# Pooled attention into a GELU MLP: value products in concurrent tiles of the PE array, and loads, pooling and DMA transposes at other places

## The chip, the cores and the metric

The kernel runs on one core of a Trainium2 chip. A core has five engines that each work through their own instruction stream in order and meet at semaphores: TensorE (PE, matrix products; its weight loads are shown apart as PEld), VectorE (DVE), ScalarE (ACT), GpSimd (POOL) and SyncE (SP, which here only starts transfers). Transfers run on 16 DMA engines. The metric is device time in microseconds (us), the median of several runs; lower is better.

## The reference

Two stages follow each other. Attention has 8 batches, 8 heads, 576 positions and 64 dimensions per head; keys and values are first averaged over blocks of 8 positions, so each head has only 72 pooled keys:

```python
k_p = k.reshape(B, H, Sp, pool, D).mean(axis=3)
v_p = v.reshape(B, H, Sp, pool, D).mean(axis=3)
scores = scale * np.matmul(q, k_p.transpose(0, 1, 3, 2))
scores = scores - np.max(scores, axis=-1, keepdims=True)
attn = np.exp(scores)
attn = attn / (np.sum(attn, axis=-1, keepdims=True) + 1e-09)
return np.matmul(attn, v_p).astype(np.float32)
```

Its output, with the heads side by side, is a matrix of 4608 rows and 512 columns, which goes through an MLP with a hidden width of 2048:

```python
h = x @ w_in
g = 0.5 * h * (1.0 + np.tanh(c * (h + 0.044715 * h * h * h)))
return (g @ w_out).astype(np.float32)
```

Inputs and output are float32. The kernel multiplies in bf16 and accumulates in float32.

## The kernel before

**Groups.** The 4608 rows are cut into nine groups of 512. Groups 0 to 7 are the first 512 positions of each batch; group R (number 8) collects the last 64 positions of all eight batches. They run in the order 0 to 6, R, 7 (`seq`). A group's MLP has a first product (16 blocks `fo` of the hidden width, each 4 matmuls over `ko`, then GELU on ACT into `gT`: `hidden`, L296 and L298) and a second product (4 row blocks `r` of 16 matmuls: `output`, L301; a copy `osb` on DVE and a store: `finish`).

**Steps and hooks.** The order of work is written out by hand. In `mlp` every matmul of a group has a step number: 0 to 63 are the first product, 64 to 127 the second. The attention of the next group is hung at step numbers with `at(hooks, step, function, ...)`, and each engine and queue gets its instructions in that order. A step only fixes the order within an engine's stream: an engine whose operands are ready runs ahead of PE, and one that waits holds up what stands behind it in its own stream. `mlp_first` does the same for group 0 with a longer numbering.

**K and V.** A tile `kv` (three buffers, shared with the staging of the weights) holds 9 chunks of 128 pooled positions by 8 by 64, in float32. The 576 = 8 x 72 pooled rows of K fill chunks 0 to 3 and the lower half of chunk 4; those of V the upper half of chunk 4 and chunks 5 to 8. `pool` adds the 8 neighbours in three halvings on DVE (L128, L129, L130) into `kvb`, in bf16. K is doubled (`dup_k`), transposed (on PE for groups 0 and 1, by a DMA transpose from SP later, L178) into `kT`, and `k_spread` copies it into `kbd`, in which each pair of heads is block-diagonal. V goes through `spread_v` on POOL (five multiplications by a mask of zeros and 0.125, L148) into `vbd`: 128-row blocks in which the columns of both heads of a pair are masked by row.

**q, scores, softmax.** q is loaded (L110), cast to `q_b` on POOL (L80) and transposed by a DMA transpose from SP (L199) into `qT`. `scores` has four matmuls per block of 128 rows, one for each pair of heads, of 144 columns (L208); for R it uses two 64-column tiles for each (L213). `exps` is one exponential on ACT (L221). `norm` sums (L228), takes the reciprocal (L230) and multiplies into `eb` (L231), on DVE for blocks 0, 2 and 3 and on POOL for block 1. Each block of `eb` is transposed into `eT` by a DMA transpose from SP (L244).

**Value products.** `values` multiplies `eT` with `vbd`. Since 72 rows per head do not fit blocks of 128, each pair of heads touches two blocks (`PARTS`): 8 full-array matmuls of 512 columns for a group (L266), 64 of 64 columns for R (L272), 16 of 256 for group 0 (L255). ACT copies the result into `xT` (L78) at step 121; seven matmuls of the second product remain behind it before the next group's first product reads `xT`.

**Where the preparation stands.** For the group stage `n_`, with next group `n` and the one after it `n2`: K and V of `n` are pooled and K is transposed in the first product (L178), scores and softmax are in the second, q of `n2` is loaded at step 57 (L570), and at step 91 q of `n2` is cast and transposed and K and V of `n2` are loaded.

**Queues.** All transfers but one go out from SP, in order: loads (L91, L93, L98, L110, L114), transposes and stores (L280, L284).

The softmax here doesn't subtract the row's maximum and nothing guards it: scores larger than these inputs give would overflow.

## Time and profile before

The median of three runs is 301.29 us (301.25 to 301.42). The execution that was profiled took 301.36 us; its span, from the first to the last instruction, is 299.3 us.

| Row of the profile | Engine | Busy us | Mean ns of one |
|---|---|---|---|
| second product L301, x560 | PE | 128.6 | 379 |
| first product L296, x640 | PE | 127.6 | 358 |
| value products L266, x56 | PE | 13.2 | 379 |
| scores L208, x128 | PE | 13.2 | 226 |
| GELU L298, x160 | ACT | 88.4 | 555 |
| spread of V L148, x40 | POOL | 21.2 | 553 |
| sums of the softmax L228, x36 | DVE | 26.5 | 736 |

The page gives busy time and idle time by groups of equal instructions. A matmul's 379 ns is its own latency; they overlap, and one of 512 columns starts 0.216 us after the other. The chain of waits is followed back from the last instruction to what released each step, and is the view for what sets the time. The timeline lists instructions by start, with their durations and, in brackets, the idle time of the engine before them and what ended it; PEq and SPq are the sequencers that issue. Transfers are listed with their time from issue to landing. Two waits of POOL and SP that the change touches stand in the list of waits: POOL's `vbd` on DVE's `kvb` 113.4 us, SP's `eT` transposes on DVE's `eb` 74.1 us. Idle time of an engine that is not on the chain costs nothing by itself.

### The profile page before, as it was taken

The page shows a single profiled execution, that of the slowest core. Times are in us where ns is not written, and L with a number is a line of the kernel's source. Part 1 is how long each engine was busy: PE and PEld are TensorE (multiplying, and loading weights), DVE is VectorE, ACT ScalarE, POOL GpSimd, SP SyncE. Part 2 cuts the span into 40 slices and gives each one's busy share as a digit, 9 for nine tenths or more (in the row PEclk, how much of TensorE's full clock was granted, in tenths as well). Part 3 has the DMA queues.
Part 4 walks back from the last instruction along what each step waited for, and adds up shares of the span by engine and source line. Part 5 has one row for each costly group of instructions (what it writes and reads, how often), then busy time and mean ns, then how long its engine had stood idle before and what let it go on. Part 6 is the DMA issues. An engine that isn't in the chain of part 4 may idle for free.

```text
span 299.3 us, 4581 instructions
## 1 busy us (share of the span) xinstructions
PE 290.7 (97%) x1734; PEld 151.6 (51%) x1734; DVE 146.7 (49%) x241; ACT 158.2 (53%) x242; POOL 55.5 (19%) x71
## 2 busy tenths in 40 slices
PE   7869999999999999999999999999999999999996
PEld 7748844445444544454445444544444544444444
DVE  6895769164706570648073807381639100920012
ACT  1477783667157715672477246724773267426500
POOL 3252033230400240024012400240024000100000
PEclk9999999999999999999999999999999999999999
DMA  7999997995699459947993599049944800351012
GB/s 235 357 387 338 384 350 132 343 279 158 135 279 250 145 127 271 269 146 126 261 297 134 119 249 301 4 107 249 276 147 101 164 36 2 79 114 37 0 70 70
DMA packets 73221, 56.32 MB, mean 188 GB/s; under 512 B 45808, under 2 KB 55408, under 8 KB 73200
## 3 DMA queue, kind: packets, MB, share of 16 engines
q1 hardware_dynamic: 73056, 55.98, 68.2%
q8 instruction: 13, 0.21, 0.3%
q10 hardware_dynamic: 144, 0.07, 0.1%
q14 instruction: 8, 0.07, 0.1%
HBM read 36.70 MB, written 9.44 MB: 154 GB/s over the span
## 4 chain that ended last, share of the span: by engine, by line
PE 91%; DMA 3%; DVE 2%; SPq 1%; POOL 1%; issue 0%; POOLq 0%
PE mm L296 41%; PE mm L301 41%; PE xo L266 4%; DMA q_sb<-in_q_dram 3%; PE sc L208 2%; PE mm L329 1%; POOL eb L231 1%; SPq L98 1%; PE xo L272 1%; PE tp L193 1%; PE sc L213 0%; DVE w_in_b L80 0%; PE tp L240 0%; DVE w_out_b L80 0%; POOL q_b L80 0%; PE xo L255 0%
## 5 line engine op out<-in xcount | busy, mean ns | idle before, releaser
L301 PE MATMUL mm<-w_out_b,gT 128*128 128x512 bf16 x560 | 128.6, 379 | 0.5 <-DVE w_out_b L80 0.5
L296 PE MATMUL mm<-xT,w_in_b 128*128 128x512 bf16 (+1 forms) x640 | 127.6, 358 | 0.5 <-DVE xT L80 0.5
L298 ACT ACTIVATE gT<-mm 128x512 bf16<-128x512 f32 (+1 forms) x160 | 88.4, 555 | 47.0 <-PE mm L296 45.9
L296 PEld LDWEIGHTS <-w_in_b 128*128 128x128 bf16 x640 | 62.2, 98 | 62.6 <-issue 0.5
L301 PEld LDWEIGHTS <-gT 128*128 128x128 bf16 x560 | 53.4, 98 | 59.7 <-DVE w_out_b L80 0.7
L80 DVE COPY osb<-mm 128x512 f32<-128x512 f32 (+2 forms) x37 | 24.3, 658 | 62.9 <-PE mm L301 60.8
L78 ACT CAST xT<-xo 128x1024 bf16<-128x1024 f32 (+1 forms) x18 | 16.6, 966 | 56.8 <-PE xo L266 49.1
L228 DVE TENSOR_REDUCE den<-e 128x8 f32<-128x576 f32 x36 | 26.5, 736 | 38.0 <-ACT e L221 37.9
L148 POOL TENSOR_TENSOR vbd<-kvb,vmask 128x256 bf16<-128x256 bf16 (+2 forms) x40 | 21.2, 553 | 113.5 <-DVE kvb L130 113.4
L128 DVE TENSOR_TENSOR kv<-kv 128x1024 f32<-128x1024 f32 (+3 forms) x20 | 22.4, 1118 | 29.7 <-DMA kv<-in_v_dram 27.7
L231 DVE TENSOR_TENSOR eb<-e,r 128x576 bf16<-128x576 f32 x28 | 27.2, 970 | 1.0
L221 ACT ACTIVATE e<-sc 128x576 f32<-128x576 f32 x36 | 22.5, 650 | 9.6 <-ACT e L221 4.0
L231 POOL TENSOR_TENSOR eb<-e,r 128x576 bf16<-128x576 f32 x8 | 10.1, 1266 | 71.5 <-ACT e L221 41.1
L80 POOL CAST q_b<-q_sb 128x2048 bf16<-128x2048 f32 (+1 forms) x7 | 15.0, 2147 | 4.1 <-DMA q_sb<-in_q_dram 4.1
L208 PEld LDWEIGHTS <-qT 128*128 128x128 bf16 x128 | 10.1, 98 | 7.0 <-ACT qT L78 0.6
L208 PE MATMUL sc<-kbd,qT 128*128 128x144 bf16 x128 | 13.2, 226 | 0.2 <-ACT qT L78 0.2
L266 PE MATMUL xo<-eT,vbd 128*128 128x512 bf16 x56 | 13.2, 379 | 0.0
L129 DVE TENSOR_TENSOR kv<-kv 128x512 f32<-128x512 f32 (+3 forms) x20 | 12.8, 640 | 0.7
L410 PE MATMUL warm<-identb 128*128 128x128 bf16 x112 | 9.1, 249 | 1.4 <-POOL vmask L398 1.4
L494 ACT ACT_TABLE_LOAD x8 | 10.3, 1283 | 0.1
L80 DVE COPY kbd<-kTd 64x288 bf16<-64x288 bf16 x12 | 5.6, 467 | 8.3 <-DMA kTd<-kvb 8.2
L314 ACT ACT_TABLE_LOAD x7 | 9.0, 1283 | 0.1
(55 smaller groups left out, 99.5 us busy)
## 6 DMA issues: line engine op xcount, KB each, us to landing
out_dram<-osb SPq DMA_DIRECT2D x31, 256.0 KB, 6.7
kv<-in_k_dram SPq DMA_DIRECT2D x7, 1024.0 KB, 6.5
q_sb<-in_q_dram SPq DMA_DIRECT2D x7, 1024.0 KB, 5.9
kv<-in_v_dram SPq DMA_DIRECT2D x7, 1024.0 KB, 9.9
w_in_s<-in_moe_w_in_dram SPq DMA_DIRECT2D x4, 1024.0 KB, 13.0
w_out_s<-in_moe_w_out_dram SPq DMA_DIRECT2D x4, 1024.0 KB, 13.8
out_dram<-osb SPq DMA_DIRECT2D x9, 128.0 KB, 2.3
kv<-in_k_dram SPq DMA_DIRECT2D x2, 512.0 KB, 3.9
```

The costliest lines, as they stand in the source:

```text
L78: eng.copy(out=out, in_=in_)
L80: eng.tensor_copy(out=out, in_=in_)
L128: add(out=t[:, :, 0:4, :], in0=t[:, :, 0:4, :], in1=t[:, :, 4:8, :], op=ALU.add)
L148: eng.tensor_tensor(out=vbd[p0:128, b, n0:n1, :].rearrange("p (c r) (hh d) -> p c (r hh) d", c=max(m, 1), d=D), in0=kvb[p0:128, 4 + c0:4 + ...
L208: nc.tensor.matmul(out=o, lhsT=qT[:, j, pr, :], rhs=kbd[:, g, pr].rearrange("d hh s -> d (hh s)"), start=True, stop=True)
L221: nc.scalar.activation(out=e.rearrange("p (x h) s -> p x (h s)", x=2), in_=sc[:, :, 0:4 * Sp], func=ACT.Exp, scale=1.0 / 64.0)
L228: nc.vector.reduce_sum(out=den, in_=e, axis=AX.X)
L231: eng.tensor_tensor(out=eb[:, j, 128 * 5 - W:].rearrange("p (h s) -> p h s", s=Sp), in0=e, in1=r.unsqueeze(2).to_broadcast([128, H, Sp]), ...
L266: nc.tensor.matmul(out=xo[:, i, :], lhsT=vbd[:, g, n, :], rhs=eT[:, :, c, :], start=(x == 0), stop=(x == 1))
L296: nc.tensor.matmul(out=hp[:, 0:c1 - c0], lhsT=w_in_b[:, ko, fo * 128:(fo + 1) * 128], rhs=st[g]["xT"][:, ko, c0:c1], start=(ko == 0), stop ...
L298: nc.scalar.activation(out=gT[:, fo, c0:c1], in_=hp[:, 0:c1 - c0], func=ACT.Gelu_apprx_tanh)
L301: nc.tensor.matmul(out=o, lhsT=gT[:, fo, r * 128:(r + 1) * 128], rhs=w_out_b[:, fo, :], start=(fo == 0), stop=(fo == FO - 1))
```

## The change

**Value products.** V is laid out by head: `vb` holds for each of 4 chunks the first 64 pooled rows of two heads, one in partitions 0 to 63, one in 64 to 127. The last 8 pooled rows of every head go to every second partition of chunk 4, mixed with the last 64 rows of K in the others. A group's product is then four matmuls on 32 rows of the array (`values_rem`), which start the sum, and eight on 64 x 64 tiles (`values_main`), four of which lie on different quarters of the array. `spread_v` is one multiplication on POOL, into `vrem`. The factor 0.125, which was in the mask, moves into the eviction (`evict`), half of which is on ACT and half on DVE. R's product does the same for each batch, in columns of 64. `eb` has another order, which takes a second, small multiplication in `norm`; `scores` writes its heads in two runs of 72 for each; the first product takes `ko` in the order 0, 2, 1, 3.

**Loads and pooling.** From group 3 on, K and V are loaded and pooled in the stage before the last one, two groups ahead: loaded at step 3 and pooled at 34 and 54 (in stage 1: 24, 92 and 107). q is loaded at 30 (57 in stage 1) and cast at 68 instead of 91. K's DMA transpose moves to step 92 (107 in stage 1), `k_spread` to step 10 of the stage after (56 for group 2, which keeps its loads and its K transpose where they were). V is now loaded in two transfers, one for each half of the partitions. R's q moves from step 92 to 110.

**The start.** The two halves of chunk 4 are loaded from ACT's queue, and the second half of V too, behind a small DVE memset that follows the first pooling.

```diff
     def load_half(b, which, eng):
+        dst = st[b]["kv"][:, 4].rearrange("(m i) pl d -> i m (pl d)", i=2)
         if which == "v":
-            eng.dma_start(out=st[b]["kv"][64:128, 4], in_=rows(v, b)[0:64])
-        else:
-            eng.dma_start(out=st[b]["kv"][0:64, 4], in_=rows(k, b)[512:576])
-    def load_main(b, which, c0, c1, eng):
-        t, w0, b0 = (k, 0, 0) if which == "k" else (v, 64, 5)
-        src = rows(t, b)[w0 + 128 * c0:w0 + 128 * c1].rearrange("(c p) pl d -> p c pl d", p=128)
-        eng.dma_start(out=st[b]["kv"][:, b0 + c0:b0 + c1], in_=src)
+            src = v[b].rearrange("h (sp pl) d -> h sp (pl d)", pl=8)[:, 64:72]
+            eng.dma_start(out=dst[0], in_=src)
+        else:
+            eng.dma_start(out=dst[1], in_=rows(k, b)[512:576].rearrange("m pl d -> m (pl d)"))
+    def load_main(b, which, c0, c1, eng, halves=(0, 1)):
+        if which == "k":
+            src = rows(k, b)[128 * c0:128 * c1].rearrange("(c p) pl d -> p c pl d", p=128)
+            eng.dma_start(out=st[b]["kv"][:, c0:c1], in_=src)
+        else:
+            for x in halves:
+                src = v[b].rearrange("h (sp pl) d -> sp h (pl d)", pl=8)[0:64, 4 * x + c0:4 * x + c1]
+                eng.dma_start(out=st[b]["kv"][64 * x:64 * x + 64, 5 + c0:5 + c1].rearrange("p c pl d -> p c (pl d)"),
+                              in_=src)
...
     def k_spread(b, engs):
+        kT = st[b]["kT"]
         for hh in range(2):
             p0 = 64 * hh
-            src = st[b]["kT"][p0:p0 + 64, 0:W].rearrange("d (pr hh s) -> d hh pr s", hh=2, s=Sp)[:, hh]
-            copy(engs[hh], kbd[p0:p0 + 64, b, :, hh, :], src)
+            src = kT[p0:p0 + 64, 0:W].rearrange("d (pr hh s) -> d hh pr s", hh=2, s=Sp)[:, hh, 0:4 - hh]
+            copy(engs[hh], kbd[p0:p0 + 64, b, 0:4 - hh, hh, :], src)
+        copy(engs[1], kbd[64:128, b, 3, 1, 0:8], kT[64:128, 504:512])
+        copy(engs[1], kbd[64:128, b, 3, 1, 8:Sp], kT[64:128, 512:640].rearrange("d (m i) -> d i m", i=2)[:, 1])
...
         sc = psum.tile([128, 2, MAIN], F32, name="sc", tag="sc", bufs=2)
         qT = st[g]["qT"]
         for pr in range(HP):
-            o = sc[:, pr // 2, 2 * Sp * (pr % 2):2 * Sp * (pr % 2) + 2 * Sp]
+            o = sc[:, pr % 2, 0:4 * Sp].rearrange("p (hh x s) -> p x hh s", hh=2, x=2)[:, pr // 2]
             if g < B:
-                nc.tensor.matmul(out=o, lhsT=qT[:, j, pr, :], rhs=kbd[:, g, pr].rearrange("d hh s -> d (hh s)"),
+                nc.tensor.matmul(out=o, lhsT=qT[:, j, pr, :], rhs=kbd[:, g, pr],
...
         nc.vector.reciprocal(out=r, in_=den)
-        eng.tensor_tensor(out=eb[:, j, 128 * 5 - W:].rearrange("p (h s) -> p h s", s=Sp), in0=e,
-                          in1=r.unsqueeze(2).to_broadcast([128, H, Sp]), op=ALU.mult)
+        eng.tensor_tensor(out=eb[:, j, 0:64 * H].rearrange("p (h s) -> p h s", s=64), in0=e[:, :, 0:64],
+                          in1=r.unsqueeze(2).to_broadcast([128, H, 64]), op=ALU.mult)
+        eng.tensor_tensor(out=eb[:, j, 64 * H:].rearrange("p (x c s i) -> p i c x s", x=2, c=4, i=2)[:, 0],
+                          in0=e[:, :, 64:Sp].rearrange("p (c x) s -> p c x s", x=2),
+                          in1=r.rearrange("p (c x) -> p c x", x=2).unsqueeze(3).to_broadcast([128, 4, 2, 8]), op=ALU.mult)
...
+    def values_rem(g, pr, o, blocks, cols):
+        p0 = 32 * pr
+        nc.tensor.matmul(out=o, lhsT=vrem[p0:p0 + 32, g].rearrange("p hh d -> p (hh d)"),
+                         rhs=st_eT[0][p0:p0 + 32, blocks, 4, cols], start=True, stop=False)
+    def values_main(g, h, o, blocks, cols):
+        r0, c0 = 64 * (h // 4), 64 * (h % 2)
+        nc.tensor.matmul(out=o[c0:c0 + 64], lhsT=vb[r0:r0 + 64, g, h % 4, :],
+                         rhs=st_eT[0][r0:r0 + 64, blocks, h % 4, cols], start=False, stop=True)
+    ORDER = [0, 1, 4, 5, 2, 3, 6, 7]
+    st_eT = [None]
+    def evict(eng, out, in_):
+        if eng is nc.scalar:
+            eng.mul(out, in_, 0.125)
+        else:
+            eng.tensor_scalar(out=out, in0=in_, scalar1=0.125, scalar2=None, op0=ALU.mult)
...
+    def values(g, engs):
+        st_eT[0] = st[g]["eT"]
+        xo = [psum.tile([128, 2, MAIN], F32, name="xo", tag="sc", bufs=2) for _ in range(2)]
+        if g < B:
+            for ko in range(KO):
+                values_rem(g, ko, xo[ko % 2][:, ko // 2, :], slice(0, 4), slice(0, 128))
+            for h in ORDER:
+                values_main(g, h, xo[h // 2 % 2][:, h // 4, :], slice(0, 4), slice(0, 128))
+        else:
+            for b in range(B):
+                cols = slice(64 * (b % 2), 64 * (b % 2) + 64)
+                for ko in range(KO):
+                    values_rem(b, ko, xo[ko % 2][:, ko // 2, 64 * b:64 * b + 64], b // 2, cols)
+                for h in ORDER:
+                    values_main(b, h, xo[h // 2 % 2][:, h // 4, 64 * b:64 * b + 64], b // 2, cols)
         for i in range(2):
...
+            evict(engs[i], st[g]["xT"].rearrange("p (y i) t -> p i y t", i=2)[:, i], xo[i])
...
-        for ko in range(KO):
-            hook(s + ko)
+        for i, ko in enumerate([0, 2, 1, 3]):
+            hook(s + i)
             nc.tensor.matmul(out=hp[:, 0:c1 - c0], lhsT=w_in_b[:, ko, fo * 128:(fo + 1) * 128],
-                             rhs=st[g]["xT"][:, ko, c0:c1], start=(ko == 0), stop=(ko == KO - 1))
+                             rhs=st[g]["xT"][:, ko, c0:c1], start=(i == 0), stop=(i == KO - 1))
...
-    load_half(0, "k", nc.sync)
-    load_half(0, "v", nc.sync)
+    load_half(0, "k", nc.scalar)
+    load_half(0, "v", nc.scalar)
     load_q(0, 0, 2, nc.sync)
-    load_main(0, "v", 0, 2, nc.sync)
-    load_main(0, "v", 2, 4, nc.sync)
+    load_main(0, "v", 0, 4, nc.sync, (0,))
     load_q(0, 2, 4, nc.sync)
...
     pool(0, 0, 2)
+    nc.vector.memset(st[0]["kv"][64:65, 5, 0, 0:1], 0.0)
+    load_main(0, "v", 0, 4, nc.scalar, (1,))
...
         at(hooks, va, nc.scalar.preload_act_table_set, GELU_SET)
-        at(hooks, va, values, n, 0, nc.scalar)
-        at(hooks, va, values, n, 1, nc.scalar)
+        at(hooks, va, values, n, [nc.scalar, nc.vector])
...
-            if kv:
-                t0 = 20 if n_ == 1 else 12
-                at(hooks, t0, pool, b, 0, 5)
-                at(hooks, t0, dup_k, b, 0, 5)
-                at(hooks, t0, kT_tile, b, None)
-                at(hooks, t0, k_transpose_dma, b)
-                at(hooks, t0 + 20, pool, b, 5, 9)
-                at(hooks, t0 + 21, spread_v, b, nc.gpsimd)
-                at(hooks, 56, k_spread, b, [nc.vector, nc.vector])
+                at(hooks, 20, pool, n, 0, 5)
+                at(hooks, 20, dup_k, n, 0, 5)
+                at(hooks, 20, kT_tile, n, None)
+                at(hooks, 20, k_transpose_dma, n)
+                at(hooks, 20, spread_v, n, nc.gpsimd)
+                at(hooks, 40, pool, n, 5, 9)
+            if n != B - 1:
+                at(hooks, 56 if n_ == 1 else 10, k_spread, kv_of(n), [nc.vector, nc.vector])
...
             if n2 != R:
-                at(hooks, 57, q_tile, n2)
-                at(hooks, 57, load_q, n2, 0, 4, nc.sync)
-            at(hooks, 91, cast_q, n2, 0, 4, nc.gpsimd)
+                at(hooks, 57 if n_ == 1 else 30, q_tile, n2)
+                at(hooks, 57 if n_ == 1 else 30, load_q, n2, 0, 4, nc.sync)
+            at(hooks, 68, cast_q, n2, 0, 4, nc.gpsimd)
             at(hooks, 91, qT_tile, n2)
             at(hooks, 91, q_transpose_dma, n2)
-            at(hooks, 91, load_kv, n2)
+            if n2 != B - 1:
+                b = kv_of(n2)
+                at(hooks, 24 if n_ == 1 else 3, load_kv, b)
+                t0, t1 = (92, 107) if n_ == 1 else (34, 54)
+                at(hooks, t0, pool, b, 0, 5)
+                at(hooks, t0, dup_k, b, 0, 5)
+                at(hooks, t0, spread_v, b, nc.gpsimd)
+                at(hooks, t1, pool, b, 5, 9)
+                at(hooks, 107 if n_ == 1 else 92, kT_tile, b, None)
+                at(hooks, 107 if n_ == 1 else 92, k_transpose_dma, b)
         if n_ == 1:
-            at(hooks, 92, q_tile, R)
+            at(hooks, 110, q_tile, R)
         if 1 <= n_ <= 4:
-            at(hooks, 92, load_q, R, n_ - 1, n_, nc.sync)
+            at(hooks, 110, load_q, R, n_ - 1, n_, nc.sync)
```

The old `values_half` and `values` go; `values_first` does for the two halves of group 0 what `values` does, with 256 columns. `load_kv` loses its test for the last batch, which moves to its caller.

## The prediction

> **What bounds the kernel now.** I read the page's engine shares first, then the chain of waits, then the timeline around one group's second product, and last the transfers with their times to landing.
>
> ```profile
> PE 290.7 (97%) x1734; PEld 151.6 (51%) x1734; DVE 146.7 (49%) x241; ACT 158.2 (53%) x242; POOL 55.5 (19%) x71
> ...
> PE 91%; DMA 3%; DVE 2%; SPq 1%; POOL 1%; issue 0%; POOLq 0%
> ```
>
> TensorE is busy almost all the time and is 91% of the chain; the rest is the first 25 us. So only PE time taken out counts, and anything that is merely moved can only cost, by making PE wait. The chain, in order of time (start, length):
>
> ```profile
> 82.22 1.73 PE xo L266 x8
> ...
> 190.98 0.25 PE sc L208 x4
> 191.23 0.43 PE mm L301 x2
> ...
> 221.33 0.37 PE sc L213 x8
> 221.71 0.54 PE mm L301 x2
> ...
> 234.90 1.87 PE xo L272 x64
> ```
>
> The value products of a group are 8 matmuls at 0.216 = 1.73 us. The rows of L213 show concurrent tiles in this very trace: eight 64-column matmuls, in pairs, take 0.37 where four full ones (L208) take 0.25, and the two L301 behind them take 0.54 instead of 0.43. So a pair costs what one costs, and the two turns (into the tiled form and out of it) cost 0.23 together, 0.11 each.
>
> Now the timeline in the stage of group 1 (its first product starts at 55.11, its second at 68.9). Here group 2's attention is prepared:
>
> ```profile
> 58.48 7.20 SPq L199 DMA_TRANSPOSE qT<-q_b  x1
> 65.77 1.22 SPq L178 DMA_TRANSPOSE kTd<-kvb  x1
> 67.04 0.58 SPq L110 DMA_DIRECT2D q_sb<-in_q_dram  x1
> 68.45 0.47 DVE L80 COPY kbd<-kTd 64x288 bf16<-64x288 bf16 x2 [3.32 <-DMA kTd<-kvb]
> ...
> 75.03 1.15 POOL L231 TENSOR_TENSOR eb<-e,r 128x576 bf16<-128x576 f32 x1 [7.64 <-ACT e L221]
> ...
> 76.12 2.42 POOL L80 CAST q_b<-q_sb 128x2048 bf16<-128x2048 f32 x1
> 76.20 4.17 SPq L244 DMA_TRANSPOSE eT<-eb  x3
> ```
>
> And its transfers (KB, us from issue to landing), the load of q in 66 to 72 us, then the transposes of the whole run:
>
> ```profile
> q_sb<-in_q_dram SPq DMA_DIRECT2D x1, 1024.0 KB, 5.6
> ...
> eT<-eb SPq DMA_TRANSPOSE x32, 2.6
> ```
>
> The reader is to see three thin margins. SP stood in one transpose for 7.20 us, until the 3.25 MB of loads and 1 MB of stores issued since 49.24 had drained (343 to 393 GB/s in every 2 us slice from 52 to 64 but one of 323). kbd was ready at 68.9 and the scores started at 69.4. The last eT transpose was issued about 79.2, landed 2.6 later at 81.8, and the values started at 82.06.
>
> **The change part by part.** The profiled run took 301.36 us: span 299.3 and 2.06 around it; the median of the runs is 301.29.
>
> *Value products of groups 1 to 7.* Four 32-row matmuls side by side count as one (0.216), eight 64x64 ones as two (0.432), plus three turns at 0.11: 0.98 instead of 1.73, a gain of 0.75. No row shows four tiles at once, nor row tiles; the pairs of L213 are nearest, and I take their behaviour. Bounds: 0.9 if a turn between two tiled forms is free, 0.15 if the 32-row matmuls run one after another.
>
> The Trainium skill's page "TensorE: Matmul & The Clock Gate", section "Measured speedup vs the span model", speaks for less: four 32-row tiles at N=512 gave 3.07 times, not 4. By it the first step would be an estimated 0.28 instead of 0.216, and the sum 0.4 us worse over six groups. "TensorEngine Tiling (Array Packing)", section "Key Properties", has the turn: a change of tiling mode drains the array; L213's 0.11 is that price here.
>
> *Group R.* 64 matmuls of 64 columns at 0.029 are 1.87. Now each of 8 batches has one round of 32-row and two of 64x64 tiles (3 x 0.029) and two turns (0.22): 8 x 0.307 + 0.11 = 2.57, 0.7 longer. Bounds +0.3 (cheaper turns) and +2.5 (12 x 8 matmuls one by one).
>
> *Group 0.* Each half: 3 x 0.108 + 0.33 = 0.65 instead of 0.86. The second half is on the chain: -0.2. The first lies in the start.
>
> *Eviction.* ACT does one copy (1.01), DVE the other (128x512 takes 0.687 and 128x256 0.425, so 1.2 for 1024), where ACT did both. Seven L301 (1.51) and two matmuls of the first product, which now takes ko 0 and 2 first, cover both. Cost nothing where DVE is free at step 121; if not, PE waits for DVE's rest.
>
> *norm.* A second multiplication of 64 elements: 0.225 by L130's 128x64 row, less 0.07 for the shorter first, +0.16 each. For n from 2 on, the cast of q leaves norm 3's side (1.36 beside it, 0.76 alone), so the last eT comes at the same time and the 0.26 of margin stays: nothing.
>
> *Scores* write in runs of 72 instead of 144; I take 0. A quarter more on each would be 36 x 0.06 = 2.2. *POOL's spread* falls from 2.8 us a group to 0.4: off the chain either way.
>
> *Loads and k's transpose from group 2 on.* SP runs ahead of PE, so K, V (2.25 MB) and q (1 MB) go one behind another at the start of the first product and need about 10 us of its 13.8; the cast of q is done before POOL is wanted at +19.9. k's transpose stands behind q's (1.9 + 1.2 us), and the loads (3 us of SP) no longer stand before the stores. DVE's waits for kTd (8.2 us in all) go. Nothing is late.
>
> *The start.* q's second half is issued about 1.7 us sooner and ahead of half of v, so the cast at 14.70 starts earlier; against it stand three small operations on DVE, one more on POOL behind L231, whose end at 22.34 releases PE, and half of v behind a DVE memset on ACT's queue. w_in's third quarter, which landed at 22.8, holds PE soon after, so there is little to gain: +0.3, between -0.5 and +1.2.
>
> *Group 2, the one that is not steady.* Four norms of group 1 are 0.16 longer each, so q, K, V of group 2 leave 0.65 later and kTd lands at 69.1; the spread has two more small copies (0.18 each by the 128x64 copies): kbd at 69.95, while PE, 0.75 ahead, is there at 68.65. It waits 1.3 us. Worse is behind it. SP now has K and V of group 3 (step 24) ahead of q of group 3 (step 57): five issues from 67.7, and 2.36 million bytes at 370 GB/s, 6.4 us, before q. q lands at 67.7 + 5.6 + 6.4 = 79.7 instead of 72.6. Its cast stands at step 68 on POOL, **ahead** of norm 1 (step 82), where it stood behind it. So: cast 79.7 to 82.0 (2.3), the two multiplications of norm 1 (1.03 + 0.3) to 83.3, then SP, which waits there with transposes 2 and 3 behind it, 1.2 each: the last is issued at 85.7 and lands at 88.3. The values start at 88.3 instead of 82.06: **+6.2**, which swallows the 1.3 and what was gained before. Bounds: if SP were not held in the transpose, the loads could follow k's transpose at once and q would land at 77, the values start at 85.6 (+3.5); with the 12.7 us that the same 3.25 MB took from 49.24, +7.
>
> *Clock.* PE then stands 5.6 us. The first 44 warm-up matmuls (128 columns) took 4.45 us and the next 22 took 1.39, so the start cost some 1.7 us of slow matmuls; PE's gap of 1.19 us at 21.2 was followed by 16 matmuls in 1.91, as before it. 5.6 us lies between these: 0.9, bounds 0 and 1.7. The granted clock reads 1.00 throughout and does not tell.
>
> The same page's "Part 1: The HAM clock gate" says that an idle window of about 3.4 us halves the clock until a busy one has passed; by it the estimate is 1.7, and the sum 0.8 higher.
>
> **Sum:** +0.3 - 0.2 + 6.2 - 6 x 0.75 + 0.7 + 0.9 = +3.4; 301.36 + 3.4 = 304.8, against the median 304.7.
>
> **The rivals.** *A, q lands in time:* then POOL is free, and DVE decides in the same stage. Its queue after the last norm (79.5) holds pooling of K3 (2.8), its copy (0.26), a copy of osb (0.69), pooling of V3 (2.4), osb (0.69): evictions start at 86.6 and end at 87.8, where the first product wants them at 85.5. It then starts at 87.4 instead of 85.46: +0.3 - 0.2 + 1.9 - 4.5 + 0.7 = -1.8, 299.5. For it: DMA moved up to 393 GB/s. Against: q cannot land before the 3.25 MB behind the transposes have moved. It decides from a landing of q at about 77.2 on, where the sum is zero, since the stall is then shorter and the clock's 0.9 falls away.
>
> *B, no wait at all:* 0.3 - 0.2 - 7 x 0.75 + 0.7 = -4.4, 296.9. For it: the waits are my reckoning of queues. Against: both orders stand in the code, and POOL, DVE and SP take theirs in order.
>
> *C, tiles of 32 rows do not run side by side:* gain 0.15 a group, R +2.5: +0.3 - 0.1 + 6.2 - 0.9 + 2.5 + 0.9 = +8.9, 310.2. For it: no row has such tiles. Against: L213's pairs start together.
>
> **How the numbers follow.** Forecast 0.55, A 0.18, B 0.12, C 0.1, others (no change among them) 0.05. The range leaves out most of B and the far end of C: 298.5 to 309; the forecast's own, by its bounds, is 301.5 to 308. This kernel's measurement tells some 0.2% from no change. Faster: B, most of A and a little of the forecast's low end, 0.28; same 0.07; slower 0.65.
>
> **What would show it.** L266's successors: a group's block of twelve in about 0.98 us. In the stage of group 1: q_sb landing near 79.7, POOL's q_b cast before its eb, and one PE gap of some 5 us before the values of group 2; later groups without gaps. A block of 1.5 us shows C; no gap and eT landed by 82 shows A or B, told apart by DVE's xT eviction. The forecast is wrong if POOL or SP get q sooner than the bytes say, or if the later groups wait too.

## The result, and the profile after

The changed kernel takes 339.55 us (median of 4 runs, 337.17 to 342.12) against 301.27 for the kernel before beside it: 1.127 times as long, with a 95% interval of 1.119 to 1.136. The forecast was 304.7, with a range up to 309. The direction was right, the size was not: 35 us are missing, and the changed kernel lies outside of every rival too. Medians here leave out the runs that took over 1.5% more than the fastest of the same kernel: two of four of v128 (its median with them, 318.4, is what some expectations reckon from), one of best1, and one of v128_all (557 us).

The profiled execution took 340.28 us, with a span of 338.6. First the page's engine shares and the head of its chain of waits:

```profile
PE 297.5 (88%) x1802; PEld 150.2 (44%) x1802; DVE 156.1 (46%) x292; ACT 150.9 (45%) x238; POOL 37.8 (11%) x46
...
PE 37%; DMA 30%; DVE 20%; SPq 7%; issue 4%; POOL 1%; ACT 0%; DVEq 0%; POOLq 0%
```

PE held 91% of the chain before; now it has 37%, and transfers have 30%. Of these, 21 points are one kind, the load of V, as the page's chain by line says. PE itself is busy longer than before (297.5 against 290.7) although the value products became cheaper: part of that time was run at a lower clock, as will be seen.

The value products do nearly what the prediction said. From the chain in order of time (start, length), group 7:

```profile
305.38 0.40 PE xo L253 x4
305.78 0.56 PE xo L258 x8
306.34 1.62 PE mm L331 x7
```

Four 32-row matmuls and eight 64x64 ones take 0.96 together, where eight matmuls took 1.73; the seven behind them take 1.62 instead of 1.51. What is lost lies in front of them. The start of each group's value product marks its stage; for the kernels of this study, in us from the span's start, each from its own timeline:

| Kernel | g1 | g2 | g3 | g4 | g5 | g6 | R | g7 | end |
|---|---|---|---|---|---|---|---|---|---|
| before | 52.14 | 82.06 | 112.41 | 142.77 | 173.12 | 203.47 | 234.73 | 265.23 | 299.3 |
| after | 60.31 | 101.61 | 137.59 | 172.24 | 207.80 | 241.71 | 273.83 | 305.38 | 338.6 |
| v128 | 52.50 | 88.59 | 121.35 | 152.27 | 182.90 | 215.00 | 247.17 | 279.13 | 312.4 |
| tiles_start | 51.65 | 80.97 | 110.75 | 140.69 | 170.38 | 200.11 | 230.64 | 262.08 | 295.3 |
| best4 | 54.85 | 84.12 | 113.91 | 143.80 | 174.21 | 203.95 | 234.48 | 265.89 | 299.2 |

From before to after, 8.2 us are lost up to group 1's values, 11.4 in the stage that follows, 3.6 to 5.6 in each of the next four, and 0.9 and 1.1 in the two behind those; behind group 7's values 0.85 is gained. The forecast had 0.1, then 6.1, then 0.9 once for the clock and, R aside, a gain of 0.75 in each.

Where the transfers went is in a table by stretches of 2 us (window, its length, busy time and instructions of PE, PEld, DVE, ACT and POOL, granted clock, share of the 16 DMA engines, GB/s), in the stage of group 2; the last two lines are of before, in its loads of 128 partitions:

```profile
112.00:114.00 2.00, 2.00 (x11) 0.94 (x10) 0.00 (x0) 1.42 (x3) 0.00 (x0) 1.00 1.06 320
114.00:116.00 2.00, 2.00 (x11) 0.93 (x10) 0.00 (x0) 1.47 (x3) 0.00 (x0) 1.00 1.05 210
116.00:118.00 2.00, 2.00 (x11) 0.88 (x9) 0.00 (x0) 1.29 (x3) 0.00 (x0) 1.00 1.05 207
118.00:120.00 2.00, 2.00 (x11) 0.89 (x10) 1.58 (x2) 1.38 (x3) 0.00 (x0) 1.00 1.09 217
...
136.00:138.00 2.00, 0.41 (x4) 0.14 (x4) 0.00 (x0) 0.00 (x0) 0.00 (x0) 0.52 0.80 154
138.00:140.00 2.00, 2.00 (x15) 0.51 (x12) 0.74 (x1) 1.02 (x1) 0.00 (x0) 0.50 1.14 212
...
58.00:60.00 2.00, 2.00 (x11) 0.94 (x10) 0.56 (x1) 1.47 (x3) 0.00 (x0) 1.00 1.04 323
60.00:62.00 2.00, 2.00 (x11) 0.89 (x10) 1.93 (x3) 1.31 (x3) 0.00 (x0) 1.00 1.05 393
```

All 16 DMA engines count as busy (1.05), as in the loads of before, but from 114 to 120, while transfers of 64 partitions run (the two halves of chunk 4, then V's two), they move 207 to 217 GB/s, where the kernel before moved 323 to 393 in its loads. The last two rows of after show the second loss: behind a gap of 4.57 us PE is granted a clock of 0.5.

What that does to group 3 is read from the timeline of DVE in the same stage:

```profile
123.43 1.23 DVE L140 TENSOR_TENSOR kv<-kv 128x1024 f32<-128x1024 f32 x1 [1.80 <-DMA kv<-in_v_dram]
...
125.76 0.74 DVE L227 TENSOR_REDUCE den<-e 128x8 f32<-128x576 f32 x1
```

V (128x1024) was issued from 109.88 on and is there at 123.4; its pooling stands at step 54, ahead of every norm, so the first sum of the softmax (L227) starts behind it at 125.76, the transposes of `eb` go out late, and PE waits for `eT`.

In the stage of group 1, q stands behind K and V of group 3 in SP's queue. From POOL's and SP's timelines:

```profile
92.89 2.13 POOL L85 CAST q_b<-q_sb 128x2048 bf16<-128x2048 f32 x1 [21.53 <-DMA q_sb<-in_q_dram]
94.99 1.04 POOL L230 TENSOR_TENSOR eb<-e,r 128x512 bf16<-128x512 f32 x1
...
96.31 3.85 SPq L246 DMA_TRANSPOSE eT<-eb  x3
```

This is the chain that the prediction laid out (q, its cast, norm 1, the transposes, the values), but q lands at 92.9 instead of 79.7, and the values start at 101.61 instead of 88.3. Of these 13 us, 8 had been lost before the stage began, in the start.

### The profile page after: what moved, and what is told of

Same layout as the page of the kernel before. It is cut to its first block, busy times and chain, and to the rows that moved or that the text cites. A ratio compares the mean times of both kernels' runs of the same rounds, so it can differ in the third digit from the quotient of the medians.

```text
span 338.6 us, 4732 instructions
## 1 busy us (share of the span) xinstructions
PE 297.5 (88%) x1802; PEld 150.2 (44%) x1802; DVE 156.1 (46%) x292; ACT 150.9 (45%) x238; POOL 37.8 (11%) x46
## 4 chain that ended last, share of the span: by engine, by line
PE 37%; DMA 30%; DVE 20%; SPq 7%; issue 4%; POOL 1%; ACT 0%; DVEq 0%; POOLq 0%
DMA kv<-in_v_dram 21%; PE mm L331 16%; PE mm L326 15%; DVE den L227 5%; DMA q_sb<-in_q_dram 4%; DMA eT<-eb 4%; DVE kv L140 3%; DVE eb L230 3%; DVE osb L85 2%; PE xo L258 2%; DVE eb L232 2%; DVE r L229 1%; SPq L109 1%; DVE kv L141 1%; PE xo L253 1%
## 5 line engine op out<-in xcount | busy, mean ns | idle before, releaser
L331 PE MATMUL mm<-w_out_b,gT 128*128 128x512 bf16 x560 | 134.2, 391 | 0.5 <-DVE w_out_b L85 0.5
L328 ACT ACTIVATE gT<-mm 128x512 bf16<-128x512 f32 (+1 forms) x160 | 88.3, 555 | 56.4 <-PE mm L326 55.4
L140 DVE TENSOR_TENSOR kv<-kv 128x1024 f32<-128x1024 f32 (+3 forms) x19 | 23.6, 1242 | 63.3 <-DMA kv<-in_v_dram 52.1
L268 ACT ACTIVATE xT<-xo 128x1024 bf16<-128x1024 f32 (+1 forms) x12 | 9.5, 812 | 83.8 <-PE xo L258 83.8
L227 DVE TENSOR_REDUCE den<-e 128x8 f32<-128x576 f32 x36 | 26.5, 735 | 34.1 <-ACT e L220 34.1
L253 PE MATMUL xo<-eT,vrem 32*128 32x64 bf16 (+2 forms) x68 | 5.8, 327 | 24.4 <-DMA eT<-eb 24.3
L270 DVE TENSOR_SCALAR xT<-xo 128x1024 bf16<-128x1024 f32 (+1 forms) x12 | 11.3, 955 | 31.7 <-PE xo L258 31.6
L230 DVE TENSOR_TENSOR eb<-e,r 128x512 bf16<-128x512 f32 x28 | 22.7, 810 | 1.0
L85 POOL CAST q_b<-q_sb 128x2048 bf16<-128x2048 f32 (+1 forms) x7 | 12.6, 1803 | 82.4 <-DMA q_sb<-in_q_dram 75.9
L156 POOL TENSOR_TENSOR vrem<-kvb,vmask 128x128 bf16<-128x128 bf16 x8 | 3.4, 422 | 117.0 <-DVE kvb L142 117.0
L230 POOL TENSOR_TENSOR eb<-e,r 128x512 bf16<-128x512 f32 x8 | 9.1, 1141 | 59.2 <-DVE r L229 53.5
L253 PEld LDWEIGHTS <-vrem 32*128 32x128 bf16 x68 | 1.9, 92 | 28.7 <-issue 28.3
L519 ACT ACT_TABLE_LOAD x8 | 10.3, 1283 | 0.1
```

Of the source, the lines that this page charges most:

```text
L85: eng.tensor_copy(out=out, in_=in_)
L140: add(out=t[:, :, 0:4, :], in0=t[:, :, 0:4, :], in1=t[:, :, 4:8, :], op=ALU.add)
L227: nc.vector.reduce_sum(out=den, in_=e, axis=AX.X)
L230: eng.tensor_tensor(out=eb[:, j, 0:64 * H].rearrange("p (h s) -> p h s", s=64), in0=e[:, :, 0:64], in1=r.unsqueeze(2).to_broadcast([128, H ...
L253: nc.tensor.matmul(out=o, lhsT=vrem[p0:p0 + 32, g].rearrange("p hh d -> p (hh d)"), rhs=st_eT[0][p0:p0 + 32, blocks, 4, cols], start=True, ...
L270: eng.tensor_scalar(out=out, in0=in_, scalar1=0.125, scalar2=None, op0=ALU.mult)
```

## The experiments

The theory after this reading: the moved transfers and steps cost as forecast, and the rest is V, whose 64-partition transfers move at little more than half the rate. The rival: the rate is as assumed, and it is the new places of the loads, the pooling and the casts that are late. Two kernels take the one without the other.

### v128: the change with V in transfers of 128 partitions

```diff
-            for x in halves:
-                src = v[b].rearrange("h (sp pl) d -> sp h (pl d)", pl=8)[0:64, 4 * x + c0:4 * x + c1]
-                eng.dma_start(out=st[b]["kv"][64 * x:64 * x + 64, 5 + c0:5 + c1].rearrange("p c pl d -> p c (pl d)"),
-                              in_=src)
+            src = rows(v, b)[64 + 128 * c0:64 + 128 * c1].rearrange("(c p) pl d -> p c pl d", p=128)
+            eng.dma_start(out=st[b]["kv"][:, 5 + c0:5 + c1], in_=src)
...
```

In the start, chunks 5 and 6 come from SP and 7 and 8, behind the memset, from ACT. V's rows land in other partitions than the products want: v128, its variants and the two tiles kernels do the work of the whole computation, but not the computation.

> The changed kernel with one thing altered: the main part of V (256 rows of 2 KB a head group) is loaded in transfers that span all 128 partitions, one for each group, instead of two transfers of 64 partitions each (for group 0 two of 128, chunks 5-6 from SP and 7-8 from ACT). V's rows come to other partitions than the value products want, so the output is not the reference's; every instruction and byte count stays. Theory H (transfers of 64 partitions move at about half the rate, 205 to 225 GB/s where the changed kernel shows them, and everything queued behind them is late): 304.7 us, 301 to 308, with the values of group 1 at about 52.5 us, no PE gap in the later groups and one of about 5 us before the values of group 2. Rival S (the new places in the order are at fault: V's pooling stands ahead of the softmax on DVE at any rate): 325 us or more, with PE gaps of 3 to 5 us before the values of every group.

Measured: 315.7 us (314.08 and 317.34), 1.049 times before [1.043, 1.055]. So some 24 of the 38.3 us are V's transfers, give or take 2 by the interval of v128: bytes, steps and, but for the start, queues are the same; the rows that V reads differ, which the next run settles. With V over 128 partitions the stage of group 1 runs as the prediction worked it out. From the timelines of POOL, SP and PE, and the last two lines from that of tiles_start, where there is no gap:

```profile
78.94 2.18 POOL L85 CAST q_b<-q_sb 128x2048 bf16<-128x2048 f32 x1 [16.44 <-DMA q_sb<-in_q_dram]
...
83.23 3.84 SPq L244 DMA_TRANSPOSE eT<-eb  x3
...
88.59 0.62 PE L251 MATMUL xo<-eT,vrem 32*128 32x512 bf16 x4 [6.84 <-DMA eT<-eb]
89.14 1.07 PE L256 MATMUL xo<-eT,vb 64*64 64x512 bf16 x8
90.14 3.04 PE L329 MATMUL mm<-w_out_b,gT 128*128 128x512 bf16 x7
93.01 3.19 PE L324 MATMUL mm<-xT,w_in_b 128*128 128x512 bf16 x14
...
110.75 0.40 PE L251 MATMUL xo<-eT,vrem 32*128 32x512 bf16 x4
...
113.15 3.19 PE L324 MATMUL mm<-xT,w_in_b 128*128 128x512 bf16 x13
```

q at 78.9 (forecast 79.7), the last eT and the values at 88.59 (88.3). Behind the wait, PE runs slowly: from the values to the first product it takes 4.42 us, against 2.40 (110.75 to 113.15) in tiles_start. But 315.7 is still 11 over the forecast; groups 3 to 6 wait too, by 1 to 2.4 us each.

### bhalf: the kernel before, with V in two transfers of 64 partitions

```diff
-        eng.dma_start(out=st[b]["kv"][:, b0 + c0:b0 + c1], in_=src)
+        for x in ((0, 64), (64, 128)) if which == "v" else ((0, 128),):
+            eng.dma_start(out=st[b]["kv"][x[0]:x[1], b0 + c0:b0 + c1], in_=src[x[0]:x[1]])
```

> The kernel before with one thing altered: every transfer of V's main part is cut into two transfers of 64 partitions (0 to 63, 64 to 127); same bytes, same places, same order. Theory H: V lands 2.5 to 3 us later in each group and, in the start, w_in too; in the steady groups V's pooling holds the copy into kbd behind it on DVE, which has about 0.5 us to spare, so 1 to 2 us for each of six groups and 3 to 6 in the start: 308 to 318 us. Rival S: 301 to 302 us, as the order is that of before.

Measured: 306.86 us (305.67 to 308.01), 1.020 [1.016, 1.022]. The rows that V reads from memory are here the same ones, in the same order, as before, and only the halves of the partitions are apart. The same table by stretches, for the 4 us in which V runs:

```profile
92.00:94.00 2.00, 1.95 (x10) 0.94 (x10) 1.31 (x1) 1.47 (x3) 0.00 (x0) 1.00 1.05 203
94.00:96.00 2.00, 2.00 (x11) 0.91 (x10) 1.76 (x4) 1.33 (x3) 0.28 (x1) 1.00 1.11 201
```

So it is the 64 partitions, not the pattern of rows. Nor is it the size of 512 KB: the two loads of K of that size in the start of before, over 128 partitions, moved 373 to 408 GB/s (from 3 to 5 us). It costs before only 5.8 us (301.0 beside it): PE loses 2.1 in four waits for `kbd`, and its first values come 2.0 later (19.43 for 17.44). The Trainium skill's page "SBUF — State Buffer", section "Door 1: The DMA port swizzle", says so: 64 partitions reach only 8 of 16 ports, and it gives 196 GB/s for 1 MiB and an asymptote of 218. The 201 to 217 here agree.

### twoq: the change with the two halves of V on two queues

```diff
-        load_main(b, "v", 0, 4, nc.sync)
+        load_main(b, "v", 0, 4, nc.sync, (0,))
+        load_main(b, "v", 0, 4, nc.scalar, (1,))
```

In the start the second half goes out from ACT as well, without the memset.

> The changed kernel with the two halves of V sent at the same time, the second from ACT's queue in every group, and in group 0 without the memset that holds it back. Theory H with two queues sharing the ports: 303 to 310 us if the halves really overlap, since the two cover all partitions together. The Trainium skill's page on SBUF states that two such transfers at once gain 6% over one; by it the time stays at 330 us or more. Rival S: 330 or more as well, so only a low time tells.

Measured: 333.49 us (332.27 to 336.02), 1.107 [1.104, 1.110], 6 less than the change: three quarters of what the halves cost stay. But it does not show what two halves at once do. In the stage of group 2 ACT, which runs ahead of SP, issued its half at 99.78 and SP its own at 108.11, behind K. So the halves ran one after the other there: 217 GB/s moved from 102 to 104, before SP's loads of K and V were issued, and 186 from 114 to 116, behind K. The same page says that two at once move 6% more than one (section "Can I just issue two DMAs to hit both halves?"); no run here shows it.

### tiles_v128 and tiles_start: the value products alone

Both put the loads, the pooling, the transposes and the casts back at the steps of before, and keep the concurrent products, with V in 128-partition transfers. tiles_v128 keeps the start of the change; tiles_start has that of before:

```diff
-    load_half(0, "k", nc.scalar)
-    load_half(0, "v", nc.scalar)
+    load_half(0, "k", nc.sync)
+    load_half(0, "v", nc.sync)
...
     load_main(0, "v", 0, 2, nc.sync)
+    load_main(0, "v", 2, 4, nc.sync)
...
-    nc.vector.memset(st[0]["kv"][64:65, 7, 0, 0:1], 0.0)
-    load_main(0, "v", 2, 4, nc.scalar)
```

> The new value products alone: V loaded over 128 partitions as in v128 (wrong rows of V, same work), and every load, pooling and transpose of K, V and q at the step where the kernel before has it. Both theories: the PE steps of the prediction without any wait, 301.3 - 0.2 - 7 x 0.75 + 0.7 + 0.3 = 296.9 us, 295.5 to 299. If it stays above 301, the gain of the tiles is lost somewhere else (eviction on DVE, norm's second multiplication).

> tiles_v128 (value products alone, V over 128 partitions, wrong rows) with the start of the kernel before: all loads of group 0 from SP, in its order, and no memset that holds half of V. Theory: in tiles_v128 the matmuls that pool V's second half waited 2.0 us for it and the first values came at 20.95 instead of 17.44, so the start costs 2.7 us by group 1: 300.8 - 2.7 = 298.1, 296.5 to 299. Rival (the start is late because of norm's second multiplication and the value products themselves): 300 to 301.

Measured: 300.78 (298.29 to 301.99) and 297.08 (297.04 to 297.83), that is 0.998 [0.995, 1.000] and 0.987 [0.985, 0.988] of before. The prediction's PE terms alone gave 296.9 (its rival B), within 0.2 us of tiles_start. The start of the change costs 3.7 us at full rate; in tiles_v128 PE waits 2.0 for V's second half from ACT's queue, and the sixteen float32 matmuls behind it (L146) then take 2.96 instead of 2.00. The forecast had 0.3 for the start. That cost is not the same in every run: tiles_v128 takes 298.29 to 301.99, and in the profiled run of v128, with the same start, PE waits only 0.5 there and the first values come at 18.29 (20.95 in tiles_v128, 17.35 in tiles_start).

### v128_cast and v128_poolv: two of the moved steps, one at a time

```diff
-            at(hooks, 68, cast_q, n2, 0, 4, nc.gpsimd)
+            at(hooks, 91 if n_ == 1 else 68, cast_q, n2, 0, 4, nc.gpsimd)
```

```diff
-                t0, t1 = (92, 107) if n_ == 1 else (34, 54)
+                t0, t1 = (92, 107) if n_ == 1 else (34, 91)
```

> v128 (V over 128 partitions, its rows at other partitions than the products want) with one step moved: in the stage of group 1, q of group 3 is cast on POOL at step 91, behind norm 1, instead of step 68. The prediction's mechanism (norm 1 of group 2 stands behind a cast that waits for q): the PE gap of 6.8 us before the values of group 2 goes, and with it the 1.9 us of slow matmuls behind it; DVE then decides there, since K and V of group 3 are pooled ahead of the eviction: a gap of 1 to 3 us at the first product of group 2. 318.4 - 8.7 + 2 = 312 us, 309 to 314. Rival (eT of group 2 is late because its transposes queue behind the 3.25 MB of loads): the gap stays above 4 us and the time at 316 or more.

> v128 with one step moved: from the stage of group 2 on, V is pooled on DVE at step 91, behind the four norms, instead of step 54, ahead of them. Theory D (in the steady groups DVE starts the softmax late because it waits for V and pools it first): the PE gaps of 1 to 2.4 us before the values of groups 3 to 7 go, 318.4 - 6 = 312 us, 310 to 315; stage 1 keeps its gap of 6.8. Rival (the cast of q beside the first norm slows DVE, or the transposes of eT wait for transfers): 316 to 319.

Measured: 312.29 (311.72 to 314.12) and 312.23 (309.82 to 313.84), both 1.036 [1.034, 1.038 and 1.032, 1.039]. From PE's waits in v128, in v128_cast and in v128_poolv (waited for, us in total, times, longest):

```profile
PE xo L251 <- DMA eT<-eb: 12.1, 5, 6.8
...
PE xo L251 <- DMA eT<-eb: 7.3, 5, 2.7
PE mm L324 <- DVE xT L268: 2.4, 1, 2.4
...
PE xo L251 <- DMA eT<-eb: 10.1, 3, 6.9
```

Each is worth some 3.4 us against v128's 315.7, not the 6 that the expectations counted from 318.4; that both times fell into their ranges is in part luck. With the cast behind norm 1 the gap of 6.84 shrinks to 0.44, and one of 2.43 appears at the first product, which waits for DVE's eviction. The stage from group 1's values to group 2's falls from 36.09 to 29.70 (before: 29.92), the 6.4 that were forecast, but the rest of the kernel takes 2.8 longer than in v128 (the 2.43 among it). With V pooled behind the norms the gap of 6.9 stays, those of the later groups fall to one of 1.91 and a few below 1.3, and the time from group 2's values to R's falls from 158.6 to 154.6. So the wait in group 2 is POOL's order, as forecast, and that in the later groups is for the most part DVE's order, V's pooling ahead of the norms, which the forecast passed over.

### v128_all: the three put right together

> The change's steps with V's main part in transfers of 128 partitions (of the wrong rows of V, as before in these kernels), the cast of q for group 2 behind norm 1 (step 91 of the second product), V pooled behind the last norm (step 91 instead of 54), and the start's transfers in the order of before on one queue. If the parts add: 318.4 less 6.1 (cast) less 6.2 (pooling) less 3.7 (start) = 302.4 (300 to 304). If all that was late had these three causes, it reaches the 297.1 of the products with the steps of before; if it stays above 306, the parts overlap.

Measured: 303.8 us (303.09 to 304.3), 1.010 [1.008, 1.012]: 11.9 below v128, where the three taken alone sum to 10.6 (3.4, 3.5 and 3.7). Given v128's interval of 2 either way, they add up. From the waits of PE:

```profile
PE xo L251 <- DMA eT<-eb: 3.8, 4, 1.7
PE mm L324 <- DVE xT L268: 3.2, 2, 2.6
```

The second row is the prediction's rival A: with q out of the way, DVE's pooling of two groups stands before the eviction, and the first product of group 2 starts at 86.82 (A had 87.4). What remains over tiles_start is 6.7 us by the medians and 6.1 by the spans (301.4 and 295.3). These two waits are 7.0 in all against 1.0 in tiles_start, which is nearly all of it; slow matmuls have no part, as the granted clock reads 1.00 behind each. Pooling two groups ahead gained nothing here over pooling where it stood.

### best1 and best3: the whole computation, with V's halves at other places

Both have the concurrent products, the start's order and the steps of before, V in two transfers of 64 partitions, and V pooled at step 57, behind `k_spread`. best3 also takes V's load out of `load_kv` and issues it behind K's transpose:

```diff
         load_half(b, "v", nc.sync)
-        load_main(b, "v", 0, 4, nc.sync)
...
                 at(hooks, t0, k_transpose_dma, b)
+                at(hooks, t0, load_main, b, "v", 0, 4, nc.sync)
...
                 at(hooks, 56, k_spread, b, [nc.vector, nc.vector])
                 at(hooks, 57, pool, b, 5, 9)
```

> A complete kernel: the new value products, V in two transfers of 64 partitions (the layout needs it), the start in the order of the kernel before, and all other loads, casts and transposes at the steps of the kernel before, except that V is pooled at step 57, behind the copy into kbd. Theory H: the halves cost 1.6 us in the start, as in bhalf, and nothing in the steady groups, since kbd no longer stands behind V on DVE: 298.1 + 1.6 = 299.7, 297 to 302. If the steady groups show gaps again, V's pooling is too late for the norms behind it: 303 to 308.

> The whole computation: concurrent value products, the steps and the start's order of before, V in two transfers of 64 partitions as in the change, but issued behind K's transpose of the same group and pooled behind k's spread, so that neither K's transpose nor q waits behind V. If V at half rate costs only through what is queued behind it: 297.1 of the products alone, plus the start, where V in halves cost 1 to 1.6 over V in one piece: 298.7 (297.5 to 300.5), faster than before. If it costs by itself (V late for its pooling, DVE held ahead of the norms), 304 to 311.

Measured: best1 310.85 (308.95 to 313.19), 1.032 [1.029, 1.036]; best3 322.75 (322.02 to 325.23), 1.073 [1.069, 1.078]. Both missed. In best1 K's transpose waits in SP's ring behind V at half rate, and PE at the scores for `kbd`; from its waits:

```profile
DVE kbd L85 <- DMA kTd<-kvb: 34.8, 6, 6.4
...
PE sc L207 <- DVE kbd L85: 9.0, 5, 3.3
```

In best3 K's transpose is free, but V lands after step 57, and DVE waits for it with all norms behind:

```profile
109.71 1.23 DVE L140 TENSOR_TENSOR kv<-kv 128x1024 f32<-128x1024 f32 x1 [6.24 <-DMA kv<-in_v_dram]
...
112.04 0.74 DVE L227 TENSOR_REDUCE den<-e 128x8 f32<-128x576 f32 x1
```

At both places the half rate was on the path.

### best4: V's halves behind K's transpose and its pooling behind the norms

```diff
-                at(hooks, 57, pool, b, 5, 9)
+                at(hooks, 91, pool, b, 5, 9)
```

> As best3 (the whole computation, V in two transfers of 64 partitions behind K's transpose), but V is pooled at step 91 of the second product, behind the last norm. If the vector engine's wait for V ahead of the norms was the whole loss of best3, the gaps before the values go and what is left over the products alone (297.1) is the start, where PE reached its first values 4.2 later: 301.3 (299.5 to 303). If q or K's transpose is late next, behind V on the ring, 305 to 312.

Measured: 301.70 us (300.63 to 303.42, 12 runs), 1.002 [1.000, 1.004], as the first theory had it. One step number is worth 21 us. V still moves at half rate (214 to 256 GB/s from 100 to 106), and nothing waits for it any more; PE's longest waits after the start are 0.7 and 0.5. From the chain's shares and PE's waits:

```profile
PE 85%; DVE 5%; DMA 4%; issue 2%; ACT 2%; SPq 2%; ACTq 0%; DVEq 0%
```

```profile
PE vp L148 <- DMA kv<-in_v_dram: 2.1, 1, 2.1
...
PE xo L253 <- DMA eT<-eb: 0.7, 1, 0.7
```

What it has over tiles_start, 3.9 us by the spans (299.2 and 295.3), is for 3.2 the start: the first values come at 20.87 instead of 17.35, behind V in halves, and group 1's at 54.85 instead of 51.65. The rest is the 0.7 before group 5's. So the gain of the concurrent products is given back there, and the whole computation ties with before.

### best5 and best6: the start of best4 in another order

best5 puts the norms of group 0 ahead of V's pooling, PE's part of that pooling behind the transposes, and 30 warming products into the gap. best6 does nearly the same and loads q's second half ahead of V's second part; its edit is shown:

```diff
-    pool(0, 5, 7)
     spread_v(0, nc.gpsimd)
-    pool_v_pe(0, 7, 9, nc.scalar)
     cast_q(0, 2, 4, nc.gpsimd)
-    warm_up(8, "mm")
+    warm_up(30, "mm")
     norm(0, 0, nc.vector)
     norm(0, 1, nc.vector)
+    pool(0, 5, 7)
...
+    load_q(0, 2, 4, nc.sync)
     load_main(0, "v", 2, 4, nc.sync)
-    load_q(0, 2, 4, nc.sync)
...
+    warm_up(10, "mm")
+    pool_v_pe(0, 7, 9, nc.scalar)
     values_first(0, [nc.vector, nc.vector, nc.scalar, nc.scalar])
```

> As best4, with the start's order changed: the first two norms of group 0 ahead of V's pooling on the vector engine, PE's part of that pooling behind the transposes of the exponentials, and 30 warming products instead of 8 in the gap. V's second part lands at 14.3; the norms no longer wait for it, so the first values come at 18 to 20 instead of 21.6: 299 (297.5 to 301) if best4 gives 301.3; the same difference of 2 to 3 below it in any case. If the rest of the start waits for V whatever the order, no difference.

> As best4, with q's second half of group 0 ahead of V's second part on the ring, the first two norms ahead of V's pooling on the vector engine, and PE's part of that pooling behind the last scores of group 0. q's second half then lands near 15, the transposes of q go at 15 to 16, V's second part lands near 17 and is pooled by 19, so the first values come at 19.2 instead of 20.9: 300.1 (299 to 301), just below before. If only the sum of the transfers counts, the first values stay at 20.9 and it gives 301.7.

Measured: 303.66 (303.54 to 304.32), 1.008 [1.007, 1.010], and 303.56 (303.02 to 304.04), 1.008 [1.007, 1.009]: both 2 us slower than best4. In best5 PE waits 3.8 for q's second half instead (18.45, `tp` on POOL's `q_b`), and the first values come at 23.88, where 18 to 20 was expected. In best6 the first values come at 20.30, only 0.57 sooner, and the stage from the second half's values to group 1's is 1.6 longer (27.42 against 25.83). The expected gain of 1.6 was not there; whether the sum of the transfers holds the start, whatever their order, two orders do not show. No version here that does the whole computation beats the kernel before.

### v4, v4_all and best2: V's rows for both halves in one transfer

To fill 128 partitions at once with the right rows, the two halves become the first dimension of one transfer, for each of the four chunks:

```diff
+            src = v[b].rearrange("(x c) (sp pl) d -> c x sp (pl d)", x=2, pl=8)
+            for c in range(c0, c1):
+                eng.dma_start(out=st[b]["kv"][:, 5 + c].rearrange("p pl d -> p (pl d)"), in_=src[c, :, 0:64])
```

v4 has this alone, v4_all with the three steps of v128_all, best2 with the steps and the start of before.

> The change whole, every row in its right place, with one thing altered: each group's main part of V comes in four transfers of 128 partitions and 256 KB, one for each pair of heads that share a place, instead of two transfers of 64 partitions and 512 KB. If the number of partitions in a transfer sets the rate, this costs what the kernel with 128-partition V and wrong rows cost, 318.4 (316 to 321). If what slowed the change's V is the strided set of rows that it reads from memory (64 of each head's 72 in one piece, the same here), it stays near 339 (335 to 342). Two more issues on SP per group are counted with 0.2 each and lie beside other work.

> The change with V in four transfers of 128 partitions, the cast of q for group 2 behind norm 1 (step 91 of the second product), V pooled behind the last norm (step 91 instead of 54), and the start's transfers in the order of before on one queue. Each was taken alone or is worked out: 318.4 for V at full rate, less 6.1 for the cast (318.4 against 312.3), less 6.2 for the pooling (318.4 against 312.2), less 3.7 for the start (300.8 against 297.1) = 302.4, if the sums add (300 to 305). If the two share one cause, the late norms, the gain of the second is smaller: 306 to 309.

> The whole computation: concurrent value products, loads, pooling and transposes at the steps of before, the start's order of before, and V in four transfers of 128 partitions with every row in its place. If only the rate of V stood between the products alone with wrong rows (297.1) and the kernel with V in halves (311.2), this gives 297.1 (296.5 to 298.5). If the strided read from memory is slow in itself, K's transpose again waits behind V and it stays at 308 to 312.

Measured: 455.22 (453.8 to 456.78), 431.51 (428.93 to 432.28) and 435.54 (434.71 to 436.59), that is 1.510 [1.506, 1.514], 1.430 [1.425, 1.435] and 1.446 [1.443, 1.449]. Neither theory had this. From best2's table by stretches, in the start, while V is moving:

```profile
14.00:16.00 2.00, 0.00 (x0) 0.00 (x0) 0.00 (x0) 0.00 (x0) 0.00 (x0) 0.50 0.13 49
16.00:18.00 2.00, 0.00 (x0) 0.00 (x0) 0.00 (x0) 0.00 (x0) 0.00 (x0) 0.50 0.13 51
```

The DMA share is 0.13 of 16, two engines, and they move 49 to 51 GB/s; a transfer of 256 KB then takes some 5 us (an estimate from that rate), and SP stands up to 7.9 us at one such issue. The first dimension of the pattern that is read has two elements. The Trainium skill's page "DMA: Bandwidth & Descriptors", section "Why a DMA increments its semaphore by 16 and not by 1", says that a transfer is split over the largest number of engines, up to 16, that divides the slowest dimension of both its patterns: with two, two engines, which is what the share shows. Other sizes of that dimension were not run here.

## Why the prediction was wrong, point by point

- *Value products 0.98 instead of 1.73:* nearly right. The chain has 0.96, but the turn out of the tiled form comes on top (1.62 for the seven matmuls behind, not 1.51), so what the 0.98 stands for, its three turns included, is 1.07. The 3.07 times of the Trainium skill's page "TensorE: Matmul & The Clock Gate" (section "Measured speedup vs the span model") would give an estimated 1.04, and is nearer. *Group R 2.57:* 2.60 in the chain (273.90 to 276.50). Rival C falls: four 32-row matmuls take 0.40 in the chain, and one after another they would take 0.86.
- *The sum of all PE terms, 296.9 (rival B):* tiles_start has 297.08, but the close fit is in part luck. B holds 0.3 for a start that tiles_start does not have; without it the terms give 296.6, and the stages of groups 1 to 5 are 0.4 to 0.7 shorter than before, not 0.75.
- *Group 2, +6.2:* right as a mechanism and, with V over 128 partitions, in size: q at 78.9 for 79.7, values at 88.59 for 88.3. In the change itself the stage, from values to values, is 11.4 longer than before where the forecast had 6.1: the price of 370 GB/s does not hold for V in halves.
- *"Loads and k's transpose from group 2 on ... need about 10 us of its 13.8 ... Nothing is late":* this is the step that failed. It took the rate of before's loads, which are of 128 partitions but for the two halves of chunk 4, for transfers that the diff cuts into 64. At 207 to 217 GB/s V's 1 MB takes about 5 us instead of under 3, and q and whatever else stands behind it in SP's ring waits along. Measured: some 24 us of 38.3. And even with V over 128 partitions something was late: V's pooling, at step 54 on DVE, stands ahead of the norms, which costs some 3.5. The prediction asked what the moved steps find on SP and POOL, but on DVE only for the stage of group 1 (rival A).
- *The start, +0.3:* 3.7 at full rate and 8.2 up to group 1's values with the halves; its bound of 1.2 was too small. V's second half, behind a memset on ACT's queue, released PE only at 19.5. The chain of after has it as one piece, in order of time:

```profile
6.03 13.44 DMA kv<-in_v_dram
```

- *Clock, 0.9 once (0 to 1.7):* 2.0 behind the gap of group 2 in v128 (4.42 against 2.40), above its upper end. In after it is paid again behind the gaps of groups 3 to 6 (4.57, 2.47, 4.19 and 2.69 us): the granted clock reads 0.50 for 2 us or more behind each. The prediction had no gap after group 2.
- *Rivals:* A's mechanism is real (v128_all: DVE releases the first product of group 2 after 2.6 us), but it only shows once the others are gone. B's time is that of tiles_start, which needs the old steps. No rival had a slower transfer, although the chances and the range rested on the rate.
- *Slips in its sums, which decide nothing:* by its own terms the gain with 32-row matmuls one after another is 0.10, not 0.15; C's 2.5 for R belongs to all twelve matmuls of a batch one by one (2.8 by its terms), and with the 32-row ones alone it is 1.4; the items of A's queue end at 86.3, not 86.6.

The 38.3 us come out as: -4.2 for the products; 11.9 for the start, the cast and the pooling taken together (3.7, 3.4 and 3.5 alone); 6.7 for what else is late with the moved steps; 23.8 for V in halves. The 11.9 and the 23.8 both rest on v128, of which two runs count, 3 us apart.

## What to carry to other kernels

When a change of layout cuts a transfer to other partitions, price it anew: the bytes are the same, and the rate is not. Behind a slow transfer, look for everything that shares its ring and for the first instruction, on an engine that works in order, that needs it; best3 and best4 differ in one step number and in 21 us. And a gain of 4 us on the busiest engine is small beside one wait of 3 us, since every wait of 2.7 us and more in these stages was paid again in slow matmuls.

## What the hardware showed that was not expected

- Where transfers of 64 partitions ran, 201 to 217 GB/s moved with all 16 engines counted busy (shares of 1.05 to 1.11): the share does not tell a full rate from a half one, the bytes do.
- Transfers whose first dimension has two elements ran on two of 16 engines, at 49 to 51 GB/s, though they fill 128 partitions.
- Four 64x64 tiles and four 32-row tiles ran at once; a group's block of twelve took 0.96, and the turn out of it some 0.11 more.
- In the stages behind the start, after idle times of PE of 2.68 to 10.3 us the granted clock read 0.50 for 2 to 5 us; after those up to 1.8 us it stayed at 1.00. Between, it did the one or the other: it fell after 2.42 in v128 and 2.47 in after, and stayed at 1.00 after 2.29 in v128_cast and 2.59 in v128_all. Behind the idle time of 6.84 in v128, seven matmuls of 512 columns took 3.04 us instead of 1.68 (tiles_start).
